# A quarter of w_mod's gate section by four transfers of four partitions, loaded at the start into the first row of the query weights, with the second key pair issued behind it

## The chip, the cores and the metric

The kernel runs on one core of one Trainium2 chip. Five engines share it: TensorE (PE, whose weight loads are shown apart as PEld), VectorE (DVE), ScalarE (ACT), GpSimd (POOL) and SyncE (SP, which here issues nearly all the transfers). Sixteen DMA engines move data between memory and the core's buffers. The metric is device time in microseconds (us). The kernel before takes 663.5 us, the median of three runs (663.39 to 663.72).

## The reference

One decode step of an adaptive-layer-norm block, with batch 4 and width 512. A vector c gives six modulation vectors of 512 numbers for each of the four rows; the attention has 32 heads of 128 and a cache of 4096 keys and values; behind it comes a small gated MLP.

```
mod = (silu(c) @ w_mod).reshape(4, 6, 1, 512)        # w_mod: 512 x 3072
sa, ca, ga, sb, cb, gb = the six slices of mod
h = layernorm(x) * (1 + ca) + sa
x = x + ga * attention(h, k_cache, v_cache, wq, wo)  # q = h @ wq; softmax(q k / sqrt(128)) v @ wo
h = layernorm(x) * (1 + cb) + sb
z = gelu(h @ w_in);  z1, z2 = halves of z;  g = w_sp * layernorm(z2) + b_sp
x = x + gb * ((z1 * g) @ w_out)
```

The last of the six slices, gb, is the gate section: columns 2560 to 3071 of w_mod. It is used only in the last line.

## The kernel before, in words

The caches are 4 x 32 x 4096 x 128 numbers of two bytes each, 134 MB for the keys and 134 MB for the values. They pass once through three buffers of 64 KB in each of the 128 partitions: bufA and bufB take the keys in turn, bufC the values. Step i of the main loop (L680) handles four heads of one batch row; steps pair up, so that one load of 8.39 MB serves two of them. The last two steps, N0 = 30 and L = 31, are handled singly, with smaller loads; the values of step 31 come in four pieces of 64, 32, 16 and 16 columns (`TAIL`, L20).

The order of the work on every engine is the order of the program text (L93, a manual schedule). A wait is put in where an instruction touches bytes that another has not finished with.

At the start (L115 to L159) the query weights (32 KB of each partition) and w_mod's first five sections go into bufC, which is free until the first values arrive. SP issues in this order: query weights, w_mod's five sections, the first key pair in two halves (`load_k(0)`), and the second key pair (`load_k(2)`, into bufB, not used before). The rows of c and x and two single numbers go by ACT's queue. From c the kernel makes cT (L254 to L264): four transposes, silu, and a cast to bf16; column j of cT holds elements j, j+4, j+8 ... of c, since w_mod is read as `(p j) n -> p j n`.

`mod_rows` (L269) multiplies cT by sections of w_mod and leaves rows; `mod_turn` (L280) transposes them to columns. Sections 0 and 1 are needed at once for h; then `queries` (L316) makes the 32 heads' queries in eight turns. Sections 2, 3 and 4 are multiplied behind the queries (L367), and turned and stored as modT by `late_mod_b` (L353), which step 0 calls behind its second multiplication.

The gate section is loaded last of all: `load_end` (L588) issues the last output weights, w_in, w_out, and then the gate section in four transfers (`KG`, L22), one for each j: 128 partitions x 1 KB. They go into `wg_sb` in bufC. At the very end of the kernel, sixteen matmuls (L870) multiply it by cT into the tile `gb`, behind the 28 matmuls of w_out (L862), whose result is y. DVE combines y with the statistics of z2 (L890 to L901) and multiplies by gb (L902). A transpose (L904), one addition (L906) and the store follow.

SP's issues at the end also wait, one by one, for a transfer some places ahead of them to land. They are the first four pieces of the last values for w_out and the gate section's first transfers.

```
    load_k(0)
    load_k(2)
    ...
        for ks in KG:
            nc.sync.dma_start(out=wg_sb[:, ks], in_=wm[:, ks, 5 * D:])
```

Of the kernel before, what the change touches and what calls it, by code (L numbers as in the profile page):

```python
# [8 lines left out]
BF16 = mybir.dt.bfloat16  # L9
F32 = mybir.dt.float32  # L10
# [8 lines left out]
RD = 8  # L19
TAIL = (64, 32, 16, 16)  # L20
KIN = (slice(0, 2), slice(2, 4))
KG = tuple(slice(k, k + 1) for k in range(4))  # L22
JW = (slice(0, 4), slice(4, 7))
RW = (slice(0, 4), slice(4, 8))

# [26 lines left out]
def kernel(  # L52
# [16 lines left out]
    nc = tc.nc  # L69
    P = 128  # L70
    B, _, D = A_x.shape
# [3 lines left out]
    DJ = D // P  # L75
# [4 lines left out]
    R = P // HQ  # L80
# [15 lines left out]
    ident_bf = front.tile([P, P], BF16, name="ident_bf")  # L96
# [3 lines left out]
    bufA, bufB, bufC = bufs  # L100
    consts = ctx.enter_context(tc.tile_pool(name="consts", bufs=1))
    wk = ctx.enter_context(tc.tile_pool(name="work", bufs=2))
    psum = ctx.enter_context(tc.tile_pool(name="psum", bufs=1, space=PSUM))
    KB = 1024
# [4 lines left out]
    def ps_sm(shape, dtype=F32):  # L109
        return psum.tile(shape, dtype, name="sm", bufs=3)  # L110

    def ps_q():
        return psum.tile([P, 512], F32, name="qps", bufs=1)
# [3 lines left out]
    pre = Arena(bufC, 52 * KB, 64 * KB)  # L117
    c_sb = pre.tile([B, D], BF16, name="c_sb")
# [5 lines left out]
    wm = w_mod.rearrange("(p j) n -> p j n", p=P)  # L124
# [21 lines left out]
    def load_k(i):  # L146
        if i < N0:
            load(bufs[i // 2 % 2], kv_view(A_k_cache, i), (NJ, NJ) if i == 0 else (NP,))
        else:
            load(kts[i], kv_view(A_k_cache, i), (NJ,))  # L150
# [5 lines left out]
            load(vts[i], kv_view(A_v_cache, i), TAIL if i == L else (NJ,))  # L156

    load_k(0)
    load_k(2)  # L159

    make_identity(nc, ident_bf)
    ident_f = consts.tile([P, P], F32, name="ident_f")
# [16 lines left out]
    def spread(n, pattern, axis, **sizes):  # L179
# [18 lines left out]
        out=far, in0=half, scalar1=-1.0, scalar2=-NEG, op0=ALU.add, op1=ALU.mult  # L198
    )
    nc.gpsimd.tensor_scalar(  # L200
        out=fars, in0=far[:, :, None].to_broadcast([P, 2, R // 2]), scalar1=-1.0, scalar2=None, op0=ALU.mult
    )
    cT = consts.tile([P, DJ, B], BF16, name="cT")
    pbd8 = consts.tile([P, NP, HP], BF16, name="pbd")
    nc.gpsimd.memset(pbd8, 0.0)
    pbds = pbd8.rearrange("p n q -> p (n q)").rearrange("p (k n q) -> p k n q", k=4, q=HQ)
# [5 lines left out]
    def rows_to_cols(src):  # L212
        t = ps_sm([P, DJ, B], BF16)
        for j in range(DJ):
            nc.tensor.transpose(t[:, j, :], src[0:B, j:D:DJ], ident_bf[0:B, 0:B])
        return t
# [34 lines left out]
        rsqrt(rs, v, 1.0, eps)  # L251
        return xc, rs

    cps = rows_to_cols(c_sb)  # L254
    cx = pre.tile([P, DJ, B], F32, name="cx")
    nc.vector.tensor_copy(out=cx, in_=cps)
    sg = pre.tile([P, DJ, B], F32, name="sg")
    nc.vector.tensor_scalar(
        out=sg, in0=cx, scalar1=-60.0, scalar2=-1.0, op0=ALU.max, op1=ALU.mult
    )  # L260
# [5 lines left out]
    mrows = pre.tile([P, D], F32, name="mrows")  # L266
# [13 lines left out]
    def mod_turn(n):  # L280
        mps = ps_sm([P, DJ, n * R])
        for j in range(DJ):
            nc.tensor.transpose(mps[:, j, :], mrows[0:n * R, j:D:DJ], ident_f[0:n * R, 0:n * R])  # L283
        return mps.rearrange("p j (s r) -> p s j r", s=n)[:, :, :, 0:B]
# [57 lines left out]

    for n in range(2 * B):
        queries(n)

    sp_t = pre.tile([1, 2], BF16, name="sp_t")
    nc.scalar.dma_start(out=sp_t[:, 0:1], in_=B_w_sp[0:1, 0:1])
    nc.scalar.dma_start(out=sp_t[:, 1:2], in_=B_b_sp.rearrange("(a b) -> a b", b=1))
    modT = consts.tile([P, 3 * DJ, B], F32, name="modT")
    g8 = consts.tile([P, 2, B], F32, name="g8")  # L350
    spf = consts.tile([P, 2], F32, name="spf")

    def late_mod_b():  # L353
        mps = mod_turn(3)
        sps = ps_sm([P, 2])
        nc.tensor.matmul(sps, lhsT=ones_b, rhs=sp_t, start=True, stop=True)
        nc.vector.tensor_copy(
            out=modT.rearrange("p (s j) b -> p s j b", s=3),
            in_=mps,
        )  # L360
        nc.vector.tensor_copy(out=spf, in_=sps)
        nc.gpsimd.tensor_copy(out=g8[:, 1, :], in_=spf[:, 0:1].to_broadcast([P, B]))
        cbT = modT[:, 2 * DJ:3 * DJ, :]
        nc.gpsimd.tensor_scalar_add(out=cbT, in0=cbT, scalar1=1.0)
# [210 lines left out]
    wol_sb = Arena(bufC, 0, 8 * KB).tile([P, HP, D], BF16)  # L575
    win_sb = Arena(bufC, 8 * KB, 22 * KB).tile([P, DJ, F], BF16)
    wout_sb = Arena(bufC, 22 * KB, 29 * KB).tile([P, NH, D], BF16)
    wg_sb = Arena(bufC, 29 * KB, 33 * KB).tile([P, DJ, D], BF16)
    tl = Arena(bufC, 33 * KB, 64 * KB)
    NL = GP * HP * DH  # L580

# [6 lines left out]
    def load_end():  # L588
        wol = A_wo[NL:H * DH].rearrange("(p r) n -> p r n", p=P)
        for rs in RW:  # L590
            nc.sync.dma_start(out=wol_sb[:, rs], in_=wol[:, rs])
        win = B_w_in.rearrange("(p j) n -> p j n", p=P)
        for ks in KIN:
            nc.sync.dma_start(out=win_sb[:, ks], in_=win[:, ks])
        for js in JW:
            nc.sync.dma_start(
                out=wout_sb[:, js],
                in_=B_w_out[js.start * P:js.stop * P].rearrange("(p j) n -> p j n", p=P),
            )
        for ks in KG:  # L600
            nc.sync.dma_start(out=wg_sb[:, ks], in_=wm[:, ks, 5 * D:])

    acc = late.tile([P, DJ, B], F32, name="acc")
    st2 = late.tile([P, 2, B, DJ + 1], F32, name="st2")
# [75 lines left out]
    for i in range(NT):  # L680
        mult(i, 0)
        if i >= 1:
            scores(i - 1)
        for k in normed_in(i - 1):
            norm_b(k)
        pick = i - 3 if i % 2 == 0 and i >= 4 else None
        if i % 2 and 3 <= i < L:
            pv(i - 2)
        if i % 2 and i < N0:
            load_v(i)  # L690
        reduce_d(i, 0)
        if pick:
            o_pick(pick)
            o_cols(pick)
        if i == L - 1:
            deal(0)
        if i == L:
            deal(2)
            pv(N0 - 1)
            load_end()  # L700
            nc.gpsimd.memset(pbd8, 0.0)  # L701
            nc.vector.memset(opss[1], 0.0)
            exps(N0)
        mult(i, 1)
        if i == 0:
            late_mod_b()
        for k in normed_in(i):
            norm_r(k)
        if pick:
            o_scale(pick)  # L710
        sum8(i, 0)
        if i == L - 1:
            dealt(0)
        if i == L:
            dealt(1)
            dealt(2)
            o_pick(N0 - 1)
            nc.vector.memset(opss[0], 0.0)
        reduce_d(i, 1)
        sum_rest(i)  # L720
        for k in normed_in(i):
            norm_a(k)
        if i == L - 1:
            deal(1)
        if i == L:
            o_cols(N0 - 1)
            project()
        if i % 2 and i + 3 < N0:
            load_k(i + 3)
        elif i == N0 - 3:  # L730
            load_k(N0)
            load_k(L)
        elif i == N0 - 1:
            load_wo()
            load_v(N0)
            late_consts()
        elif i == N0:
            load_v(L)
# [89 lines left out]
    def gate(h, part):  # L828
# [26 lines left out]
        out=zz.rearrange("p f g b -> p g b f"), in0=z1[:, None].to_broadcast([P, 2, B, NH]),  # L855
        in1=st3[:, 0:2], op=ALU.mult,
    )
    y = ps_q()[:, 0:DJ * 2 * B].rearrange("p (j g b) -> p j g b", j=DJ, g=2)
    for js in JW:
        for j in range(DJ):  # L860
# [3 lines left out]
                    start=(j == 0 and f == 0), stop=(f == NH - 1), skip_group_check=True,  # L864
                )

    gb = ps_sm([P, DJ, B])
    for k in range(DJ):
        for j in range(DJ):
            nc.tensor.matmul(  # L870
                gb[:, j, :], lhsT=wg_sb[:, k, j * P:(j + 1) * P], rhs=cT[:, k, :],
                start=(k == 0 and j == 0), stop=(k == DJ - 1), skip_group_check=True,
            )
    mq3 = tl.tile([P, 2, B], F32, name="mq3")
    nc.vector.tensor_reduce(
# [62 lines left out]
```

## Time and profile before

| what | value |
|---|---|
| median of three runs | 663.5 us (663.39 to 663.72) |
| the profiled execution | 663.53 us |
| its span | 661.7 us |
| DVE busy | 570.8 us, 86% |
| PE busy | 316.3 us, 48% |
| ACT busy | 172.0 us, 26% |
| POOL busy | 19.4 us, 3% |
| bytes moved by DMA | 283.07 MB, mean 428 GB/s |
| mean granted clock of TensorE | 0.747 |

The span is the time from the first to the last thing that the profiler recorded; the execution's own time is 1.83 us longer. The page's line "DMA" gives, for 40 equal slices of the span, the mean busy share of the 16 DMA engines in tenths (9 is 90% or more). A transfer is recorded as packets, each with a queue (q1 is SP's, q10 is ACT's, q8 and q14 carry instructions for the engines themselves), a start, a size and a duration; every DMA engine that takes part in a transfer writes a packet of four bytes when its share is done. In the timeline a row is: start, duration, engine, line, operation, output and inputs, count, and in brackets the idle time before it and what ended it.

### The profile page before, as it was taken

The page shows a single profiled execution, that of the slowest core. Times are in us where ns is not written, and L with a number is a line of the kernel's source. Part 1 is how long each engine was busy: PE and PEld are TensorE (multiplying, and loading weights), DVE is VectorE, ACT ScalarE, POOL GpSimd, SP SyncE. Part 2 cuts the span into 40 slices and gives each one's busy share as a digit, 9 for nine tenths or more (in the row PEclk, how much of TensorE's full clock was granted, in tenths as well). Part 3 has the DMA queues.
Part 4 walks back from the last instruction along what each step waited for, and adds up shares of the span by engine and source line. Part 5 has one row for each costly group of instructions (what it writes and reads, how often), then busy time and mean ns, then how long its engine had stood idle before and what let it go on. Part 6 is the DMA issues. An engine that isn't in the chain of part 4 may idle for free.

```text
span 661.7 us, 5060 instructions
## 1 busy us (share of the span) xinstructions
PE 316.3 (48%) x2064; PEld 134.6 (20%) x2064; DVE 570.8 (86%) x368; ACT 172.0 (26%) x284; POOL 19.4 (3%) x56
## 2 busy tenths in 40 slices
PE   1565363635154463514446351444535254453885
PEld 0122121212021121202112120111212022121444
DVE  3239999999898998989899898979979898999943
ACT  1220505033060603206060330605023060503322
POOL 3000000000000000000000000000000000030100
PEclk9998787867678785767878576787856778775975
DMA  8999999999999999999999999999999999999996
GB/s 364 447 427 444 440 441 440 441 405 436 440 433 440 444 433 412 445 432 432 437 440 437 424 436 428 433 440 440 429 432 433 428 440 441 420 422 451 414 417 280
DMA packets 8060, 283.07 MB, mean 428 GB/s; under 512 B 860, under 2 KB 1380, under 8 KB 2916
## 3 DMA queue, kind: packets, MB, share of 16 engines
q1 hardware_dynamic: 8016, 282.73, 99.0%
q8 instruction: 16, 0.26, 0.1%
q14 instruction: 8, 0.07, 0.0%
q10 hardware_dynamic: 20, 0.01, 0.0%
HBM read 282.73 MB, written 0.00 MB: 427 GB/s over the span
## 4 chain that ended last, share of the span: by engine, by line
DMA 70%; PE 14%; DVE 10%; ACT 4%; issue 1%; POOL 0%; SPq 0%; ACTq 0%; DVEq 0%
DMA bC<-in_A_v_cache_dram 54%; PE ops L510 11%; DMA bA<-in_A_k_cache_dram 6%; DMA bC<-in_A_wo_dram 4%; DVE S L401 4%; DMA bC<-in_w_mod_dram 4%; DVE bA L381 3%; ACT pbd L455 3%; PE red L389 2%; DMA bC<-in_B_b_sp_dram 2%; DVE bB L381 1%; DVE S L412 1%; PE qps L331 1%; PE sm L323 1%; ACT qbp L341 0%
## 5 line engine op out<-in xcount | busy, mean ns | idle before, releaser
L455 ACT ACTIVATE pbd<-S,nb 32x256 bf16<-32x256 f32 x120 | 154.3, 1520 | 422.6 <-DVE nb L442 421.3
L381 DVE TENSOR_TENSOR bA<-bA,qbp 128x8192 bf16<-128x8192 bf16 x32 | 142.4, 4451 | 21.7 <-DMA bA<-in_A_k_cache_dram 21.7
L389 PE MATMUL red<-bB,ident_bf 128*128 128x512 bf16 x344 | 97.2, 441 | 113.6 <-DVE bB L381 113.6
L389 PE MATMUL red<-bA,ident_bf 128*128 128x512 bf16 x332 | 93.3, 440 | 110.2 <-DVE bA L381 110.2
L389 PEld LDWEIGHTS <-ident_bf 128*128 128x128 bf16 x676 | 72.8, 110 | 337.7 <-issue 175.5
L381 DVE TENSOR_TENSOR bB<-bB,qbp 128x8192 bf16<-128x8192 bf16 x28 | 123.7, 4418 | 13.4 <-DMA bB<-in_A_k_cache_dram 13.4
L510 PE MATMUL ops<-bC,pbd 128*32 128x512 bf16 x960 | 83.6, 525 | 69.9 <-DMA bC<-in_A_v_cache_dram 64.8
L401 DVE TENSOR_REDUCE S<-bA 128x48 f32<-128x6144 bf16 x15 | 98.1, 6543 | 0.0
L401 DVE TENSOR_REDUCE S<-bB 128x48 f32<-128x6144 bf16 x14 | 91.6, 6542 | 0.0
L510 PEld LDWEIGHTS <-pbd 128*32 128x32 bf16 (+1 forms) x1016 | 37.4, 126 | 120.5 <-issue 63.9
L455 ACT ACTIVATION_READ_ACCUMULATOR pbd<-S,nb 32x1 f32 x120 | 58.8, 490 | 0.0
L412 DVE TENSOR_REDUCE S<-red 128x64 f32<-128x512 f32 x64 | 43.7, 683 | 4.4 <-PE red L389 4.3
L469 POOL TENSOR_TENSOR rsb<-maskd,rs 128x8 f32<-128x8 f32 x15 | 3.8, 253 | 556.9 <-ACT pbd L455 556.9
L381 DVE TENSOR_TENSOR bB<-bB,qbo 128x8192 bf16<-128x8192 bf16 x4 | 17.6, 4410 | 0.0
L522 DVE TENSOR_REDUCE osb<-ops 128x128 f32<-128x512 f32 x17 | 11.8, 692 | 0.6
L519 DVE TENSOR_TENSOR ops<-ops,m 128x512 f32<-128x512 f32 x15 | 10.4, 693 | 0.0
L295 DVE SCALAR_TENSOR_TENSOR bC<-sm,bC 128x16 f32<-128x16 f32 x1 | 0.2, 175 | 11.4 <-PE sm L283 11.4
L488 PE MATMUL sm<-rsb,inv_d 128*128 128x32 f32 (+2 forms) x12 | 2.9, 338 | 14.6 <-POOL rsb L469 14.6
L273 PE MATMUL sm<-bC,cT 128*4 128x512 bf16 x20 | 3.7, 621 | 8.4 <-DMA bC<-in_w_mod_dram 8.4
L455 ACT ACTIVATE pbd<-S,nM 32x128 bf16<-32x128 f32 x8 | 4.6, 576 | 12.1 <-POOL pbd L701 10.9
L425 DVE TENSOR_REDUCE mrow<-S 128x1 f32<-128x256 f32 (+1 forms) x17 | 6.9, 404 | 0.6
L331 PE MATMUL qps<-bC 128*128 128x256 bf16 (+1 forms) x16 | 4.5, 383 | 4.1 <-ACT qbp L341 2.8
(159 smaller groups left out, 134.0 us busy)
## 6 DMA issues: line engine op xcount, KB each, us to landing
bA<-in_A_k_cache_dram SPq DMA_DIRECT2D x2, 4096.0 KB, 31.4
bB<-in_A_k_cache_dram SPq DMA_DIRECT2D x2, 4096.0 KB, 41.6
bC<-in_A_wq_dram SPq DMA_DIRECT2D x1, 4096.0 KB, 12.3
bA<-in_A_v_cache_dram SPq DMA_DIRECT2D x1, 4096.0 KB
bA<-in_A_wo_dram SPq DMA_DIRECT2D x1, 3072.0 KB
bC<-in_w_mod_dram SPq DMA_DIRECT2D x1, 2560.0 KB, 18.0
bB<-in_A_v_cache_dram SPq DMA_DIRECT2D x1, 2048.0 KB, 32.3
bC<-in_B_w_in_dram SPq DMA_DIRECT2D x2, 896.0 KB
```

Of the source, the lines that this page charges most:

```text
L323: nc.tensor.matmul(qr[R * q:R * (q + 1)], lhsT=hT[:, k, :], rhs=wq_v[:, k, gs, q, :], start=(k == 0), stop=(k == DJ - 1), tile_position=(0 ...
L331: nc.tensor.matmul(qp[:, 0:npair], lhsT=eb2[k][:, b].rearrange("p k q r -> p (k q r)"), rhs=qrow[:, h, k:2 * npair:2], start=(k == 0), sto ...
L381: nc.vector.tensor_tensor(out=kt, in0=kt, in1=bc(q, KC), op=ALU.mult)
L389: nc.tensor.matmul(red, lhsT=ident_bf, rhs=kt[:, :, m * rd:(m + 1) * rd], start=(m == 0), stop=(m == DH // rd - 1),)
L401: nc.vector.tensor_reduce(out=st[i, "S"][:, n0:NJ], in_=kts[i][:, n0:NJ, :], axis=AX.X, op=ALU.add)
L412: nc.vector.tensor_reduce(out=st[i, "S"][:, kc * KC:kc * KC + on_pe(i, kc)], in_=st.pop((i, "red", kc)), axis=AX.X, op=ALU.add,)
L425: nc.vector.tensor_reduce(out=mrow, in_=S, axis=AX.X, op=ALU.max)
L455: nc.scalar.activation(out=pbd8[r, :, 2 * q + h] if pair(i) else pbds[r, i % 4, :, q], in_=S[r, :], func=AF.Exp, bias=nM[r, h:h + 1], scal ...
L469: nc.gpsimd.tensor_tensor(out=st["P", g, "rsb"][:, b], in0=maskd[:, :, None].to_broadcast([P, HQ, 2]), in1=rs[:, None, :].to_broadcast([P, ...
L510: nc.tensor.matmul(ops_of(i)[g:g + rows], lhsT=pb[:, n, :], rhs=vt[:, n, :], start=(m < 4), stop=(m >= end - 4), tile_position=(0, g),)
L519: nc.vector.tensor_tensor(out=ops, in0=ops, in1=sel[:, :, None].to_broadcast([P, G, DH]), op=ALU.mult)
L522: nc.vector.tensor_reduce(out=osb, in_=ops.rearrange("p g d -> p d g"), axis=AX.X, op=ALU.add)
```

## The change

The gate section has 512 rows. The first 384 are still loaded at the end, now in three transfers (`KE` = 3) of 128 partitions x 1 KB. The other 128 rows are loaded at the start: 16 partitions (`PU`) of 8 rows (`RU`) each, that is 8 KB for each of 16 partitions, into the place where the first row (j = 0) of the query weights has been. Four transfers carry them, the b-th with partitions b, b+4, b+8 and b+12. They are issued by SP behind the queries in the program text, and `load_k(2)` is moved from the head of the kernel to stand behind them.

cT gets 15 columns in place of 4: the old four, three for the 384 rows in their new order, and eight for the 128 rows, of which only 16 partitions are used (the rest of the tile is cleared by POOL). That makes fifteen transposes in place of four, and two copies out of PSUM in place of one. In step 0 a new function, `mod_uneven`, multiplies the 128 rows' part with eight matmuls of 512 columns into rows 96 to 99, and ACT copies it to `mrows` with its columns reordered; `late_mod_b` turns four sections in place of three, and modT becomes a third larger. At the end one f32 matmul with the identity puts that part into `gb`, now ahead of y's matmuls, and twelve matmuls in place of sixteen add the rest behind y.

```diff
-KG = tuple(slice(k, k + 1) for k in range(4))
+KE = 3
+RU = 8
+EV = 128 * KE
+PU = 16
+KG = tuple(slice(k, k + 1) for k in range(KE))
...
     load_k(0)
-    load_k(2)
+    wgu_sb = Arena(bufC, 0, RU * KB).tile([P, RU, D], BF16)[0:PU]
...
-    cT = consts.tile([P, DJ, B], BF16, name="cT")
+    NC = DJ + KE + RU
+    cT = consts.tile([P, NC, B], BF16, name="cT")
...
-    cps = rows_to_cols(c_sb)
-    cx = pre.tile([P, DJ, B], F32, name="cx")
-    nc.vector.tensor_copy(out=cx, in_=cps)
-    sg = pre.tile([P, DJ, B], F32, name="sg")
+    cps = ps_sm([P, NC, B], BF16)
+    cuts = [slice(j, D, DJ) for j in range(DJ)]
+    cuts += [slice(k, EV, KE) for k in range(KE)] + [slice(EV + r, D, RU) for r in range(RU)]
+    for n, cut in enumerate(cuts):
+        pn = P if n < DJ + KE else PU
+        nc.tensor.transpose(cps[0:pn, n, :], c_sb[0:B, cut], ident_bf[0:B, 0:B])
+    cx = pre.tile([P, NC, B], F32, name="cx")
+    nc.gpsimd.memset(cx[:, DJ + KE:], 0.0)
+    nc.vector.tensor_copy(out=cx[:, 0:DJ + KE], in_=cps[:, 0:DJ + KE])
+    nc.vector.tensor_copy(out=cx[0:PU, DJ + KE:], in_=cps[0:PU, DJ + KE:])
+    sg = pre.tile([P, NC, B], F32, name="sg")
...
     for n in range(2 * B):
         queries(n)
+    wu = w_mod[EV:D, 5 * D:].rearrange("(p r) n -> p r n", r=RU)
+    for b in range(4):
+        nc.sync.dma_start(out=wgu_sb[b:PU:4], in_=wu[b:PU:4])
+    load_k(2)
...
-    modT = consts.tile([P, 3 * DJ, B], F32, name="modT")
+    modT = consts.tile([P, 4 * DJ, B], F32, name="modT")
...
+    def mod_uneven():
+        mp = ps_sm([P, D])
+        for r in range(RU):
+            nc.tensor.matmul(
+                mp[3 * R:3 * R + B], lhsT=cT[0:PU, DJ + KE + r, :], rhs=wgu_sb[:, r, :],
+                start=(r == 0), stop=(r == RU - 1), tile_position=(0, 3 * R),
+            )
+        nc.scalar.copy(
+            out=mrows[3 * R:3 * R + B].rearrange("b (p j) -> b j p", j=DJ),
+            in_=mp[3 * R:3 * R + B].rearrange("b (j p) -> b j p", j=DJ),
+        )
...
-        mps = mod_turn(3)
+        mps = mod_turn(4)
...
-    wg_sb = Arena(bufC, 29 * KB, 33 * KB).tile([P, DJ, D], BF16)
+    wg_sb = Arena(bufC, 29 * KB, 33 * KB).tile([P, KE, D], BF16)
...
+        wge = w_mod[0:EV, 5 * D:].rearrange("(p k) n -> p k n", p=P)
         for ks in KG:
-            nc.sync.dma_start(out=wg_sb[:, ks], in_=wm[:, ks, 5 * D:])
+            nc.sync.dma_start(out=wg_sb[:, ks], in_=wge[:, ks])
...
         if i == 0:
+            mod_uneven()
             late_mod_b()
...
+    gb = ps_sm([P, DJ, B])
+    nc.tensor.matmul(
+        gb.rearrange("p j b -> p (j b)"), lhsT=ident_f, rhs=modT[:, 3 * DJ:4 * DJ, :].rearrange("p j b -> p (j b)"),
+        start=True, stop=False, skip_group_check=True,
+    )
     y = ps_q()[:, 0:DJ * 2 * B].rearrange("p (j g b) -> p j g b", j=DJ, g=2)
...
-    gb = ps_sm([P, DJ, B])
-    for k in range(DJ):
+    for k in range(KE):
         for j in range(DJ):
             nc.tensor.matmul(
-                gb[:, j, :], lhsT=wg_sb[:, k, j * P:(j + 1) * P], rhs=cT[:, k, :],
-                start=(k == 0 and j == 0), stop=(k == DJ - 1), skip_group_check=True,
+                gb[:, j, :], lhsT=wg_sb[:, k, j * P:(j + 1) * P], rhs=cT[:, DJ + k, :],
+                start=False, stop=(k == KE - 1), skip_group_check=True,
             )
```

More of the change, by code (lines that the diff above doesn't have):

```diff
@@ L357, in late_mod_b @@
         nc.vector.tensor_copy(
-            out=modT.rearrange("p (s j) b -> p s j b", s=3),
+            out=modT.rearrange("p (s j) b -> p s j b", s=4),
             in_=mps,
```

## The prediction

> **What bounds the kernel now.** I read the page's DMA lines first, then the DMA packet records of the trace, then the timeline at both ends, then the chain that ended last.
>
> ```profile
> span 661.7 us, 5060 instructions
> ...
> DMA  8999999999999999999999999999999999999996
> ...
> q1 hardware_dynamic: 8016, 282.73, 99.0%
> q8 instruction: 16, 0.26, 0.1%
> q14 instruction: 8, 0.07, 0.0%
> q10 hardware_dynamic: 20, 0.01, 0.0%
> ```
>
> SP's transfers (q1) fill the 16 DMA engines from 1.7 us to the last slice. In the packet records each 8.39 MB load ends 19.32 us after the one before it (57.07, 76.39, 95.71 ... 578.68 on the earliest engine): no gap anywhere. So work on the other engines in the middle costs nothing; a byte in the stream does.
>
> The 16 engines are not level. The four-byte completion packets of a transfer lie 0.48 us apart at 37.75 us, but 3.33 us apart at 634.38 us. Each step is one instruction-fetch packet: a q8 fetch (16 KB) puts its engine back 1.42 us, a q14 fetch (8 KB) 0.55 to 0.85 us. The 16 q8 fetches go round eight engines; the other eight get only the q14 ones. Now to the engines that matter. The loads of c and x (4 rows of 1 KB each) have left 4 data and 4 completion packets each, and the two one-element loads 2 each: 8 + 8 + 4 = the 20 of q10. So a four-partition load ran on four engines. Matching the x packets to the q1 packets on either side, those four had, at 37.75 us, the offsets 0.00, 0.02, 0.11 and 0.30 us. Followed to 634.38 us, they are at 0.00, 1.13, 0.13 and 2.83 us. The last, which I call engine R, took q14 fetches at 103.26, 345.58 and 625.77 us. The latest engine of all is at 3.33.
>
> Timeline of the last 25 us (start, duration, engine, line, [idle before, releaser]):
>
> ```profile
> 638.06 1.03 PE L510 MATMUL ops<-bA,pbd 128*16 128x512 bf16 x8 [0.49 <-DMA bA<-in_A_v_cache_dram]
> ...
> 642.96 1.44 PE L510 MATMUL ops<-bB,pbd 128*16 128x512 bf16 x16 [0.67 <-DMA bB<-in_A_v_cache_dram]
> ...
> 645.41 0.61 PE L510 MATMUL ops<-bB,pbd 128*16 128x512 bf16 x8 [0.69 <-DMA bB<-in_A_v_cache_dram]
> ...
> 646.63 0.56 PE L544 MATMUL qps<-pbd,bB 128*128 128x4 bf16 x16 [0.61 <-DMA bB<-in_A_v_cache_dram]
> ...
> 655.96 0.68 PE L220 MATMUL sm<-bA 128*128 128x56 f32 x2
> ...
> 656.61 0.89 PE L862 MATMUL qps<-bC 128*128 128x8 bf16 x28
> ...
> 657.35 1.19 PE L870 MATMUL sm<-cT,bC 128*128 128x4 bf16 x16
> ...
> 657.53 0.19 DVE L890 TENSOR_TENSOR bC<-g,qps 128x32 f32<-128x32 f32 x1 [0.18 <-PE qps L862]
> ...
> 658.24 0.17 DVE L901 TENSOR_TENSOR bC<-bC 128x16 f32<-128x16 f32 x1
> ...
> 658.58 0.17 DVE L902 TENSOR_TENSOR bC<-bC,sm 128x16 f32<-128x16 f32 x1 [0.16 <-PE sm L870]
> ```
>
> Each piece of the last V load ends a PE wait; behind the third there are 12 us of dependent compute. Two paths meet at L902: that compute (L901 ends 658.41) and w_mod's gate section, whose last packet ends 657.90. The chain shows how:
>
> ```profile
> 650.42 7.81 DMA bC<-in_w_mod_dram
> 658.23 0.04 issue
> 658.27 0.28 PE sm L870 x4
> 658.55 0.02 issue
> 658.58 0.18 DVE bC L902
> ```
>
> The transfer path wins by about 0.13 us only. And the landing of the last V pieces is set by the **latest** of the 16 engines.
>
> **The change part by part.** Sum against the profiled execution: 663.53 us, span 661.7 and 1.83 around it; the median is 663.5.
>
> *Tail, 128 KB less.* In the packet records an engine takes 0.345 us for one of the four gate transfers (8 packets of 1 KB and a completion). With one fewer, the last packet of an unmoved engine ends at 657.55. At L902 this can return at most the 0.13 us by which that path leads.
>
> *Front, 128 KB more.* Four transfers of four partitions, 8 rows of 1 KB for each. By the x row, each runs on four engines, the same four: 4 x 8 = 32 packets of 0.043 us and 4 completions, 32/8 x 0.345 = 1.38, say 1.40 us on each of four engines and nothing on twelve. The Trainium skill, "DMA: Bandwidth & Descriptors", section "Why a DMA increments its semaphore by 16 and not by 1", has this as a rule: the engine count is the largest k up to 16 that divides the slowest dimension on both sides, on SP and ACT queues the lowest-numbered k. The 20 packets of q10 agree. Three of the four engines have room (0.00, 0.13, 1.13, with 1.40 added still under 3.33). Engine R hasn't: 2.83 + 1.40 = 4.23. Until 617 us R is at 1.99 + 1.40 = 3.39, level with 3.33, so the middle does not move. From V's last two transfers on, R sets the landings:
>
> ```
> completion, us      earliest engine   engine R   latest   R + 1.40
> V of step 30                 634.38     637.21   637.71     638.61
> V of step 31, piece 1        639.25     642.08   642.57     643.48
> piece 3                      642.95     645.79   646.28     647.19
> piece 4                      644.20     647.03   647.53     648.43
> gate section, last           654.58     657.40   657.90     658.80 (658.46 with one transfer less)
> ```
>
> Each landing is 0.90 us later. PE waits for each of them today (0.49, 0.67, 0.69, 0.61 us, all ended by the DMA), so the compute moves by the whole 0.90: **+0.90 us**.
>
> *The last gate product.* Four L870 matmuls go (4 x 0.026 us, behind y; not on the path any more). In their place one f32 matmul with ident_f stands **before** the 28 y matmuls (L862). The f32 matmul of the same kind at L550 takes 0.447 us from its start to the start of the bf16 matmul behind it (647.541 to 647.986). L220's pair lets its follower load weights at 656.215 and finish that at 656.485; y began at 656.608, when DVE had made zz. With the new one from 656.485, y starts at 656.93: +0.32 us, which DVE's L890 to L901 pass on whole. Bounds: 0 if it fits the gap, 0.45 if nothing overlaps. I take 0.32, as the rows around it give it. L901 then ends at 658.73 and L902 starts at about 658.77, 0.19 us later than today, no longer held by the gate section: **+0.19 us**. With the 0.90 the gate's last product is ready near 659.2, still ahead of DVE at 659.63.
>
> *The move of the second key pair (SP's queue).* It now waits behind four transfers that wait for the last reader of the query weights' row 0: the first four of the second L323 group (29.99 us, 16 matmuls in 1.90 us), so about 30.6. Row 0 alone counts: at the end the output weights' first half is issued at 622.64 into the first 8 KB of a buffer whose other part PE reads until 625.8. Four issues at 0.4 to 0.65 us and the pair's own 0.48 end by 33.7. Issue to first packet is 1.03 us (0.73 to 1.76), so the pair is there by 34.7. The stream reaches it at 37.75 on the earliest engine: 3 us of cover, **cost 0**; without the cover see the rivals. Behind it on SP is the first V load, issued at 48.30 and needed at 57.07: 8 us of cover.
>
> *Front compute, all covered.* Eleven more transposes and one more DVE copy, a POOL clear behind the 1.81 us clear at 3.54, wider sigmoid: cT later by some 2 us, xn with it (11.9 to about 14); PE waits for w_mod until 19.21. Eight more row products (L273: 8 in 1.87 us), one ACT copy (0.58) and wider transposes fall between 42.3 and 48.0, where PE waits for the one-element loads. Without that cover PE would be 3 us later at step 0, while the stream stays the bound: 0.
>
> Sum: 663.53 + 0.90 + 0.19 = 664.62, against the median **664.6 us**, 0.17% longer.
>
> **Rivals.** My bound for no change is 0.2%, about what a measurement of this kernel can tell: 662.2 to 664.8.
>
> *A hole in the stream (slower).* If the four transfers wait for all query work (PE L336 ends 36.31) and not for row 0, four issues (1.8 us) and 1.03 us put the pair's first packet at 39.1, against 37.75: a hole of 1.35 us for the whole stream, in which R's extra packets hide. 663.53 + 1.35 + 0.19 = 665.1. It decides from a hole of 1.15 us on. For it: SP is in order. Against: the 622.64 issue.
>
> *Even spread.* If 32 rows are dealt over 16 engines, each is 0.35 later in front: 663.53 + 0.35 + 0.19 = 664.1. The x load had only four rows and can't exclude it.
>
> *R not late.* If R's third fetch moves behind V, R is at 3.39, landings hold, and 663.53 + 0.19 = 663.7. R's fetch stands in the trace at 625.77; which instruction calls it, no view says.
>
> *Small gain.* The f32 matmul fits the gap and R isn't late: 663.53 - 0.13 = 663.4. A gain over 0.2% has no place to come from: L901 at 658.41 stands.
>
> *Each small transfer pays a start.* If the four engines idled 1.03 us (issue to first packet) ahead of each, R would be 4.1 later still: 668.7. The gate transfers, as small per engine, follow each other without a gap, which speaks against it. The Trainium skill, "DMA: Bandwidth & Descriptors", section "Rules for kernel authors", says that transfers under 64 KB are mostly overhead; these are 32 KB.
>
> **How the numbers follow.** Forecast 0.57 (664.2 to 665.0: L550's bounds and 0.2 us on the landings), hole 0.13, even spread 0.10, R not late 0.11, small gain 0.05, starts 0.04. The range 663.6 to 665.5 leaves out the small gain, the starts, and the upper part of the hole. Slower by over 0.2% (above 664.83): the hole, the starts, and a third of the forecast, whose middle lies only 0.2 us below the bound: 0.36. Faster by over 0.2%: no case gives it; 0.04 for what I don't see. Same: 0.60.
>
> **What would show it.** In the packets: 128 more of 1 KB near 38 us on four engines, 128 fewer at the end; completions of the V pieces some 0.9 us further apart. In the timeline: L544's DMA wait ends near 647.5; y starts at 657.8; L902 is no longer released by PE. The second pair's packets follow the first's without a gap, or there is the hole. I am wrong if those four engines are not the x load's four, or if R's fetch is elsewhere.

## The result and the profile after

The changed kernel takes 664.79 us (median; 664.53 to 665.19), the kernel before in the same series 663.46 us: ratio 1.0020, 95% interval 1.0013 to 1.0027. It is slower by 1.33 us, which lies just inside the 0.2% (664.83) that the prediction took as its bound for no change. The forecast was 664.6, with a range of 663.6 to 665.5. The profiled execution took 664.66 us, 1.13 us more than that of before.

The page of the changed kernel, at its span, the DMA line of part 2 and part 3:

```profile
span 662.9 us, 5104 instructions
...
DMA  8999999999999999999999999999999999999996
...
q1 hardware_dynamic: 8016, 282.73, 98.8%
q8 instruction: 16, 0.26, 0.1%
q14 instruction: 8, 0.07, 0.0%
q10 hardware_dynamic: 20, 0.01, 0.0%
```

Bytes and packets are what they were; the stream still fills every slice, and the span has grown by 1.2 us. So the time isn't in the amount of work. The timeline of SP's queue about the moved load (start, duration, queue, line):

```profile
30.61 2.80 SPq L359 DMA_DIRECT2D bC<-in_w_mod_dram  x4
33.45 0.44 SPq L147 DMA_DIRECT2D bB<-in_A_k_cache_dram  x1
```

The four transfers are issued from 30.61 us, as soon as row 0 of the query weights is read, and the second key pair at 33.45. In the packet records, 128 packets of 1 KB run from 37.73 to 39.30 us, 32 on each of exactly four engines; the other twelve go from the first key pair to the second (first packet at 37.69) with nothing between. No hole.

The last 25 us of the changed kernel, from the timeline (lines answer to those of before as L510 to L538, L544 to L572, L862 to L897, L870 to L904, L890 to L924, L901 and L902 to L935 and L936, and the MLP's first matmul L836 to L866; L889 is new):

```profile
638.92 1.03 PE L538 MATMUL ops<-bA,pbd 128*16 128x512 bf16 x8 [1.45 <-DMA bA<-in_A_v_cache_dram]
...
643.77 1.30 PE L538 MATMUL ops<-bB,pbd 128*16 128x512 bf16 x16 [0.61 <-DMA bB<-in_A_v_cache_dram]
...
646.22 0.61 PE L538 MATMUL ops<-bB,pbd 128*16 128x512 bf16 x8 [0.83 <-DMA bB<-in_A_v_cache_dram]
...
647.43 0.56 PE L572 MATMUL qps<-pbd,bB 128*128 128x4 bf16 x16 [0.60 <-DMA bB<-in_A_v_cache_dram]
...
654.76 1.86 PE L866 MATMUL red<-bC 128*128 128x4 bf16 x56 [1.04 <-DVE bC L845]
...
656.70 0.68 PE L225 MATMUL sm<-bA 128*128 128x56 f32 x2
...
657.17 0.57 PE L889 MATMUL sm<-modT,ident_f 128*128 128x16 f32 x2
...
657.57 0.89 PE L897 MATMUL qps<-bC 128*128 128x8 bf16 x28
...
659.21 0.17 DVE L935 TENSOR_TENSOR bC<-bC 128x16 f32<-128x16 f32 x1
...
659.49 0.17 DVE L936 TENSOR_TENSOR bC<-bC,sm 128x16 f32<-128x16 f32 x1
...
660.44 0.36 SPq L941 DMA_DIRECT2D out_dram<-bC  x1
```

Two rows of the timeline of before that belong beside these:

```profile
654.02 1.86 PE L836 MATMUL red<-bC 128*128 128x4 bf16 x56 [0.98 <-DVE bC L815]
...
659.53 0.36 SPq L907 DMA_DIRECT2D out_dram<-bC  x1
```

Against before, the four waits for V pieces end 0.86, 0.81, 0.81 and 0.80 us later (638.06, 642.96, 645.41 and 646.63 there). The MLP's first matmul (L866) starts 0.74 later, y 0.96, L935 0.97, L936 0.91, and the store's issue 0.91. So most of the loss is made by 638.9 us, in the landings; about 0.2 more is added between L866 and y: 2.81 us from the one to the other, 2.59 before.

The end of the chain that ended last, of the changed kernel (start, duration, what):

```profile
657.37 0.36 PE sm L889 x2
657.73 0.74 PE qps L897 x28
658.50 0.20 DVE bC L924
...
659.21 0.18 DVE bC L935
...
659.49 0.18 DVE bC L936
```

The transfer of w_mod's gate section, 7.81 us of the chain before, is gone from it; the new f32 product L889 is in it, and L936 has no releaser any more.

The completions in the packet records say which engine holds the landings. Step 30's V load, 16 engines (us):

```
before   earliest 634.38 ... 637.21 (R) ... 637.49, 637.71
after    earliest 634.50 ... 637.53, 637.60, 638.45 (R)
```

Engine R, whose fetches stand at 102.08, 346.82 and 625.79 us here, has gone from a place in the pack to the last by 0.85 us. Its packets can be followed one by one. At the end of the first key pair R is at 37.91 us here and at 38.05 before, so it starts 0.14 earlier. Its share of the four small transfers ends at 39.29, 1.38 later. At the second key pair it is 1.24 behind its place before (58.61 against 57.37), and at 638.45 still 1.24; the three fetches cost it the same in both kernels.

One part of the loss appears only behind the store. The store is issued 0.91 us later, the profiled execution ends 1.13 later. At the end of the program SP waits for its semaphores one by one, in a fixed order. Its records (start, us; the store's own is marked):

```
before   659.935  659.999  660.061  660.125  660.919 (store's)  done 660.984
after    660.850 (store's, lasts 0.977)  661.863  661.925  661.989  662.051  done 662.116
```

The transfers of SP and ACT take eight semaphores in turn (the records name them), and with another number of transfers the store has another one. Before, four waits were passed while the store was under way and its own came behind them; after, the store's comes first and four of 0.063 us follow it: from issue to done 1.45 us before, 1.68 after, some **0.22 us** that no view of the profile lists.

So the profiled difference has three terms: landings +0.74 (as L866 feels them), the product before y +0.22 with 0.06 returned because L902 no longer waits for the gate section, and the order of the last waits +0.22. Their sum is 1.12, against 1.13. The medians differ by 1.33, with an interval of 0.9 to 1.8 us; the 0.2 between the two figures is within it and isn't traced.

### The profile page after: what moved, and what is told of

It is laid out like the page before. It is cut to its first block, busy times and chain, and to the rows that moved or that the text cites. A ratio compares the mean times of both kernels' runs of the same rounds, so it can differ in the third digit from the quotient of the medians.

```text
span 662.9 us, 5104 instructions
## 1 busy us (share of the span) xinstructions
PE 318.2 (48%) x2081; PEld 135.0 (20%) x2081; DVE 569.9 (86%) x369; ACT 173.2 (26%) x285; POOL 19.5 (3%) x57
## 4 chain that ended last, share of the span: by engine, by line
DMA 61%; DVE 21%; PE 13%; ACT 2%; issue 1%; SPq 0%; ACTq 0%; DVEq 0%
DMA bC<-in_A_v_cache_dram 40%; DMA bA<-in_A_k_cache_dram 12%; PE ops L538 8%; DVE S L429 7%; DVE bA L409 7%; DMA bB<-in_A_v_cache_dram 5%; DVE bB L409 3%; PE red L417 3%; DMA bC<-in_w_mod_dram 3%; DMA bC<-in_B_b_sp_dram 2%; ACT pbd L483 2%; DVE S L440 1%; PE qps L343 1%; PE sm L335 1%; DVE osb L550 0%
## 5 line engine op out<-in xcount | busy, mean ns | idle before, releaser
L417 PE MATMUL red<-bA,ident_bf 128*128 128x512 bf16 x332 | 94.8, 446 | 109.1 <-DVE bA L409 109.1
L538 PE MATMUL ops<-bC,pbd 128*32 128x512 bf16 x960 | 81.8, 516 | 69.5 <-DMA bC<-in_A_v_cache_dram 60.7
L538 PEld LDWEIGHTS <-pbd 128*32 128x32 bf16 (+1 forms) x1016 | 36.4, 124 | 120.2 <-issue 63.1
L550 DVE TENSOR_REDUCE osb<-ops 128x128 f32<-128x512 f32 x17 | 11.8, 692 | 0.6
```

What stands on the lines that cost most here:

```text
L417: nc.tensor.matmul(red, lhsT=ident_bf, rhs=kt[:, :, m * rd:(m + 1) * rd], start=(m == 0), stop=(m == DH // rd - 1),)
L538: nc.tensor.matmul(ops_of(i)[g:g + rows], lhsT=pb[:, n, :], rhs=vt[:, n, :], start=(m < 4), stop=(m >= end - 4), tile_position=(0, g),)
L550: nc.vector.tensor_reduce(out=osb, in_=ops.rearrange("p g d -> p d g"), axis=AX.X, op=ALU.add)
```

## The experiments

My theory after the comparison: the landings are late because the four-partition transfers put 1.4 us on four engines, one of them R, while the same bytes on other engines cost nothing; the product costs 0.22; the last waits cost 0.22 to 0.25. The rivals: the load costs in front, whichever engines carry it (even spread, or a hole); or the loss comes from the tail's new compute. Times below are medians with those of the kernel before on the same chip.

| experiment | us | before | difference | ratio, 95% interval |
|---|---|---|---|---|
| load alone, four transfers | 664.69 | 663.59 | +1.10 | 1.0007 to 1.0025 |
| half the rows, four engines | 664.10 | 663.64 | +0.46 | 0.9998 to 1.0016 |
| half the rows, two engines | 664.06 | 663.59 | +0.47 | 0.9998 to 1.0016 |
| product earlier | 664.48 | 663.64 | +0.84 | 1.0004 to 1.0022 |
| store's semaphore alone | 663.88 | 663.59 | +0.29 | 0.9995 to 1.0012 |
| engine R alone | 664.30 | 663.59 | +0.71 | 1.0002 to 1.0020 |
| one transfer | 664.95 | 663.64 | +1.31 | 1.0011 to 1.0028 |
| load alone, one transfer, adjacent | 664.96 | 663.59 | +1.37 | 1.0011 to 1.0029 |
| load alone, one transfer, spread | 664.43 | 663.59 | +0.84 | 1.0004 to 1.0021 |
| six transfers | 668.12 | 663.64 | +4.48 | 1.0054 to 1.0079 |
| eight transfers of two partitions | 669.33 | 663.59 | +5.74 | 1.0073 to 1.0101 |
| the same, product earlier | 668.99 | 663.59 | +5.40 | 1.0068 to 1.0096 |

An interval is about 1 us wide, so differences of a few tenths between two experiments are read from their traces, not from this table.

### The load alone

The kernel before, its tail untouched, with four transfers like the change's in front of the second key pair; what they bring is not read, and the whole gate section still comes at the end.

```
-    load_k(2)          # behind load_k(0)
     for n in range(2 * B):
         queries(n)
+    wgu_sb = Arena(bufC, 0, 8 * KB).tile([P, 8, D], BF16)[0:16]
+    wu = w_mod[3 * P:D, 5 * D:].rearrange("(p r) n -> p r n", r=8)
+    for b in range(4):
+        nc.sync.dma_start(out=wgu_sb[b:16:4], in_=wu[b:16:4])
+    load_k(2)
```

> The kernel before with one part of the change alone: the four transfers of four partitions in front, behind the queries, with the second key pair behind them. The 128 rows are loaded twice, nothing reads the first copy. Theory: R ends step 30's values 0.74 us later than the latest did, as in the changed kernel; L902 waits for R's last gate packet, near 659.4; the store's semaphore is checked first, 0.22: 0.9 to 1.0 us longer, 664.4 us. Rival (the front load is hidden, the compute edits cost the time): 663.5 to 663.7 us.

It came out 1.10 us longer. The timeline of this kernel at the V waits and at the meeting of the two paths:

```profile
638.76 1.03 PE L514 MATMUL ops<-bA,pbd 128*16 128x512 bf16 x8 [0.80 <-DMA bA<-in_A_v_cache_dram]
...
647.27 0.56 PE L548 MATMUL qps<-pbd,bB 128*128 128x4 bf16 x16 [0.61 <-DMA bB<-in_A_v_cache_dram]
...
659.14 0.17 DVE L906 TENSOR_TENSOR bC<-bC,sm 128x16 f32<-128x16 f32 x1 [0.19 <-PE sm L874]
```

The V waits end 0.70 and 0.64 us later than before, and the gate section's matmuls (L874) release L906 as they released L902. The load alone, without any of the new compute, makes most of the loss (0.80 us in the profiled execution, where the change shows 1.13). The four extra transfers have also moved the store's semaphore to the front of the last waits, as in the change.

### Half the rows, on four engines or on two

Both bring 64 rows instead of 128 and leave the other 64 out. The first halves what each of the four engines gets; the second keeps 32 packets per engine but uses two partitions for a transfer.

```
     for b in range(4):
-        nc.sync.dma_start(out=wgu_sb[b:PU:4], in_=wu[b:PU:4])
+        nc.sync.dma_start(out=wgu_sb[b:PU:4, 0:RU // 2], in_=wu[b:PU:4, 0:RU // 2])
```
```
-        nc.sync.dma_start(out=wgu_sb[b:PU:4], in_=wu[b:PU:4])
+        nc.sync.dma_start(out=wgu_sb[b:8:4], in_=wu[b:8:4])
```

> The changed kernel with the four transfers kept, each carrying four of its eight rows per partition; the other 64 rows of the gate section are left out. Theory: engine R gets 16 packets, 0.70 us instead of 1.40, ends step 30's values at 637.75, just behind the others at 637.60: 0.70 us earlier, 664.1 us. Rival (each small transfer has a cost of its own, not its packets): four transfers as before, 664.8 us.

> The changed kernel with four transfers of two partitions, 8 rows each: 64 packets on two engines, 32 on each, so those two carry what each of four carries in the changed kernel; the other 64 rows of the gate section are left out. No more transfers than in the changed kernel, so no later second key pair. Theory (R alone sets the landings): if R is not among the two, the latest engine ends step 30's values at 637.60 and the time is 0.85 us below the changed kernel, 0.5 us above the one before. If R is one of the two: as the changed kernel, 1.3 us above. Rival (32 packets of 1 KB on any engine in front are enough): 1.3 us above, with R not carrying any.

Both are some 0.47 us above before, about what the product and the last waits cost by themselves. In the second the packets are on exactly two engines, 32 on each, as many per engine as in the change (their second key pair begins at 39.10 and 39.35 us). Step 30's V load is complete at 637.74 us, against 637.71 before and 638.45 in the changed kernel; in the first at 637.80. From the timeline of the two-engine kernel:

```profile
645.47 0.61 PE L538 MATMUL ops<-bB,pbd 128*16 128x512 bf16 x8 [0.20 <-DMA bB<-in_A_v_cache_dram]
...
646.65 0.57 PE L572 MATMUL qps<-pbd,bB 128*128 128x4 bf16 x16 [0.57 <-DMA bB<-in_A_v_cache_dram]
```

The last V wait ends at 646.65, and at 646.63 before. So 1.4 us of packets in front cost nothing at the end when the engines that carry them are not the late one. That R isn't among these two shows in the packets: the engine that takes the fetch at 103.14 us, R's by its time (103.26 before, 102.08 in the change), is then 0.3 us behind the earliest engine, and the two that carried the packets are 1.5 and 1.7 behind. That speaks against the rivals in which the load costs by its place in front: with half the bytes they would have half the loss in the landing, which moved by 0.03 us. The first of the two kernels fits as well: R with half the load is at 2.83 + 0.70 = 3.53 by the prediction's working, only 0.20 behind the latest engine of before.

### The product earlier

The f32 product stands ahead of the MLP's first matmuls, where PE waits for DVE.

```
+    gb = ps_sm([P, DJ, B])
+    nc.tensor.matmul(
+        gb.rearrange("p j b -> p (j b)"), lhsT=ident_f, rhs=modT[:, 3 * DJ:4 * DJ, :].rearrange("p j b -> p (j b)"),
+        start=True, stop=False, skip_group_check=True,
+    )
     x1s = tl.tile([B * DJ, P], F32, name="x1s")
...
-    gb = ps_sm([P, DJ, B])
-    nc.tensor.matmul(
-        gb.rearrange("p j b -> p (j b)"), lhsT=ident_f, rhs=modT[:, 3 * DJ:4 * DJ, :].rearrange("p j b -> p (j b)"),
-        start=True, stop=False, skip_group_check=True,
-    )
     y = ps_q()[:, 0:DJ * 2 * B].rearrange("p (j g b) -> p j g b", j=DJ, g=2)
```

> The changed kernel with the f32 identity product moved from ahead of y's matmuls to ahead of the MLP's first matmuls, where PE waits for DVE. Theory: y starts as soon as zz is made, 0.22 us earlier, and L935 ends that much earlier: 664.55 us. Rival (the product fits a gap of PE and costs nothing): 664.8 us.

Timeline of this kernel:

```profile
653.92 0.61 PE L854 MATMUL sm<-modT,ident_f 128*128 128x16 f32 x2
655.02 1.85 PE L871 MATMUL red<-bC 128*128 128x4 bf16 x56 [0.49 <-DVE bC L845]
...
657.60 0.89 PE L897 MATMUL qps<-bC 128*128 128x8 bf16 x28
```

From the first MLP matmul to y it is 2.58 us, as before the change (2.59), against 2.81 with the product in its place. L871 still waits 0.49 us for DVE, so the product is covered. Its price is 0.22 to 0.23. In this profiled execution R's landing was 638.72, 0.27 later than in the changed kernel's, so the spans don't show the gain; the intervals of the medians don't separate it either.

### The store's semaphore, and engine R alone

First: the kernel before with three one-element loads on ACT's queue at the start, which move the store to another semaphore and do nothing else. Second: the change, with the product early as above, and five such loads, so that the store's semaphore is waited for last.

```
     nc.scalar.dma_start(out=x_sb, in_=A_x.rearrange("b s d -> (b s) d"))
+    spare = pre.tile([1, 4], BF16, name="spare")
+    for k in range(3):
+        nc.scalar.dma_start(out=spare[:, k:k + 1], in_=B_w_sp[0:1, 0:1])
```
```
+    spare = pre.tile([1, 8], BF16, name="spare")
+    for k in range(5):
+        nc.scalar.dma_start(out=spare[:, k:k + 1], in_=B_w_sp[0:1, 0:1])
```

> The kernel before with three more one-element loads at its start, on ACT's queue, into bytes that nothing reads. The count of transfers is then that of the changed kernel, and the store gets the semaphore that SP checks first at the end, with four more checks behind it. Theory: 0.22 us longer, 663.68 us. Rival (what the span shows behind the store is chance): 663.46 us.

> The changed kernel with its two smaller costs taken away: the f32 product ahead of the MLP, and five more one-element loads at the start, so that the store gets the semaphore that SP checks last. Theory (three terms: engine R, the product 0.22, the final checks 0.25): only engine R is left, 0.8 to 0.9 us above the kernel before. Rival (the terms do not add, another cost hides behind): over 1.1 us above.

In the first, SP's first wait ends at 661.10 us and four more follow, to 661.36: the order is that of the changed kernel. The time is 0.29 longer, but its interval (-0.3 to +0.8 us) holds nothing as well, so the time alone doesn't show the 0.22; the records of SP do (1.68 us from the store's issue to done, as in the changed kernel). In the second the first waits are passed between 660.486 and 660.676 us and the store's own ends last, at 661.45 (1.45 us from issue to done, as before). What is left of the change there is R: 638.34 for the latest completion, and from its timeline

```profile
638.81 1.03 PE L541 MATMUL ops<-bA,pbd 128*16 128x512 bf16 x8 [1.06 <-DMA bA<-in_A_v_cache_dram]
...
654.64 1.84 PE L874 MATMUL red<-bC 128*128 128x4 bf16 x56 [0.50 <-DVE bC L848]
...
657.20 0.89 PE L900 MATMUL qps<-bC 128*128 128x8 bf16 x28
```

the first V wait 0.75 us later than before, L874 0.62 later, y 0.59. The whole is +0.71 us. Adding the product (0.22) and the last waits (0.22) gives 1.15, near the 1.13 of the profiled executions and the 1.33 of the medians (0.9 to 1.8 us by the interval). Within the intervals, the terms add.

### The same rows by one transfer

If four engines are the trouble, all sixteen should be the cure: one transfer of sixteen partitions puts eight packets on each engine.

```
-    for b in range(4):
-        nc.sync.dma_start(out=wgu_sb[b:PU:4], in_=wu[b:PU:4])
+    nc.sync.dma_start(out=wgu_sb, in_=wu)
```

> The changed kernel with its quarter sent by one transfer of 16 partitions instead of four of four. Theory (engine R carries 32 packets and sets V's landings): 8 packets, 0.35 us, fall on every engine; R ends the load of step 30's values at 637.4 instead of 638.45 and the other late engines at 637.95, so the landings come 0.50 us earlier. With three transfers fewer the store's semaphore is again the last that SP checks: another 0.22 us. 664.79 - 0.72 = 664.05 us. Rival (a longer stream or SP's wait in front costs the time, not one engine): only the 0.22 goes, 664.55 us.

A miss: 1.31 us over before, no better than the change. The V load of step 30 was complete at 639.11, later than with R alone. I then gave the kernel before such a load by itself, once into sixteen adjacent partitions and once into every eighth; nothing reads it.

```
-    load_k(2)          # behind load_k(0)
     for n in range(2 * B):
         queries(n)
+    wgu_sb = Arena(bufC, 0, 8 * KB).tile([P, 8, D], BF16)
+    wu = w_mod[3 * P:D, 5 * D:].rearrange("(p r) n -> p r n", r=8)
+    nc.sync.dma_start(out=wgu_sb[0:16], in_=wu)       # second kernel: wgu_sb[0:P:8]
+    load_k(2)
```

> The kernel before with only a front load added: one transfer of 16 adjacent partitions (0 to 15), 8 packets of 1 KB on each engine, behind the queries with the second key pair behind it; nothing reads it. In the one-transfer run every engine's first packet of the second key pair took 3.0 to 3.4 us instead of 2.42. If that comes from 16 engines writing 16 adjacent partitions, it is here again: 0.35 + 0.8 us on every engine, and two checks behind the store's (0.13): 1.2 to 1.3 us above the kernel before. If it was chance: 0.35 + 0.13, 0.5 us above.

> The same with the one transfer's 16 partitions eight apart (0, 8 ... 120), the same packets and bytes. Theory (adjacent partitions are what is crowded): the first key packets take 2.42 us, 0.5 us above the kernel before. Rival (1 KB packets on all 16 engines at once in mid-stream are slow wherever they go): as with adjacent partitions, 1.2 us above.

From the packet records (us; "pair done" is the second key pair's completions on the engines, with one later engine in brackets):

```
                        1 KB packet   first 64 KB of an engine   pair done               V of step 30
changed kernel              0.046             2.42               57.00 (earliest)           638.45
one transfer                0.056          2.55 to 3.36          58.01 to 58.52 (60.38)     639.11
load alone, adjacent        0.062          2.88 to 3.71          58.14 to 59.15 (59.82)     639.35
load alone, every eighth    0.048          2.57 to 2.72          57.59 to 58.17 (59.68)     638.48
```

With one transfer, not only the small packets are slow, but the first 64 KB packets of the key pair behind them: all sixteen engines lose time there, 0.1 to 0.9 us each (0.5 to 1.3 with the load alone). The packets behind these take 2.42 us again. With the partitions eight apart the slowing is smaller but still there (+0.84 us in all, between the two values that I had expected). So by the packets adjacency is most of it and not all; the intervals of the two medians overlap.

The slowing isn't peculiar to transfers into sixteen partitions. The first packets of the query weights at the start of the kernel, 32 KB each, took 1.23 to 2.18 us before the change, and later ones of that size 1.21. Behind the hole of the six transfers below, the first 64 KB packets took 2.93 to 3.36 us. In each of these cases all sixteen engines come to large packets anew; in the changed kernel twelve of them go straight on from the first key pair, and nothing is slowed. What the engines contend for isn't shown, and stays open.

### Six transfers, and eight of two partitions

Two more transfers in the same manner, into partitions that nothing reads, should put 0.69 us more on R. Eight transfers of two partitions should take the rows to two engines without R.

```
         nc.sync.dma_start(out=wgu_sb[b:PU:4], in_=wu[b:PU:4])
+    wgx_sb = Arena(bufC, 0, RU * KB).tile([P, RU, D], BF16)[PU:2 * PU]
+    for b in range(2):
+        nc.sync.dma_start(out=wgx_sb[b:PU:4], in_=wu[b:PU:4])
```
```
-    for b in range(4):
-        nc.sync.dma_start(out=wgu_sb[b:PU:4], in_=wu[b:PU:4])
+    for b in range(8):
+        nc.sync.dma_start(out=wgu_sb[b:PU:8], in_=wu[b:PU:8])
```

> The changed kernel with two more transfers of four partitions of the same rows, into 16 partitions that nothing reads. Theory: 16 packets more on the four engines, 0.70 us, all of it on V's landings since R is the latest already: R ends step 30's values at 639.15. The store's semaphore moves from the first to the second wait, 0.06 us back: 665.4 us. Rival (the landings are not what moved the end): 664.8 us. Rival (SP too late for the second key pair): SP issues 1.4 us more, the pair is there near 36.5, still ahead of 37.7, no hole.

> The changed kernel with eight transfers of two partitions instead of four of four: all 128 packets on two engines, 64 each, 2.76 us. Theory: if R is not one of the two, R ends step 30's values at 637.05, and the two, which take few or no fetches, stay below the others at 637.60: landings 0.85 us earlier, and the store's semaphore is checked fourth instead of first (0.19): 663.75 us. If R is one of the two: 1.36 us later, 666 us. Rival (SP): eight issues of 0.7 us end near 36.2, the second key pair's first packet comes near 37.7, just when the stream needs it; a hole would be some tenths at most.

> Both edits together on the changed kernel: two engines (eight transfers of two partitions) and the f32 product ahead of the MLP. Theory: 663.75 - 0.22 = 663.5 us, level with the kernel before, since its compute path to L901 was only 0.13 us ahead of the gate section. Rival (the moved quarter is worth more than 0.13 us once it is off engine R): below 663.3 us.

The last is the eight transfers with the product early, as above. All three missed by several microseconds, for one reason. The timeline of the kernel with six transfers, SP's queue and then the last V wait:

```profile
30.62 2.79 SPq L359 DMA_DIRECT2D bC<-in_w_mod_dram  x4
33.45 5.69 SPq L362 DMA_DIRECT2D bC<-in_w_mod_dram  x2
40.28 0.34 SPq L147 DMA_DIRECT2D bB<-in_A_k_cache_dram  x1
...
651.20 0.56 PE L575 MATMUL qps<-pbd,bB 128*128 128x4 bf16 x16 [0.63 <-DMA bB<-in_A_v_cache_dram]
```

The sixth issue waited until 38.52 us, because its semaphore, one of the eight, belonged to the second half of the first key pair, which was complete only at 38.50. The key pair behind it then waited for the next semaphore in turn, that of a one-element load of ACT's queue, which landed at 40.27. So it was issued at 40.28 instead of 33.45, its first packet is at 41.25 instead of 37.7, and for about 3.5 us the stream of the caches stood still. SP's waits in this kernel show both (us in total, how often, the longest):

```profile
SPq L362 <- DMA bA<-in_A_k_cache_dram: 4.4, 1, 4.4
...
SPq L147 <- DMA bC<-in_B_w_sp_dram: 1.1, 1, 1.1
```

The last V wait ends 3.8 us later than in the changed kernel: the hole arrives whole at the end. With eight transfers the sixth issue waits so until 38.78 us and the seventh, for the one-element load, until 40.26:

```profile
30.70 10.83 SPq L359 DMA_DIRECT2D bC<-in_w_mod_dram  x8
41.58 0.40 SPq L147 DMA_DIRECT2D bB<-in_A_k_cache_dram  x1
```

The pair's first packet is at 42.61, a hole of 4.9 us, and the span is 4.8 us longer than the changed kernel's. The early product takes 0.34 off again, within the intervals. So none of these kernels tells anything of R, and the two-engine question had to be put again with four transfers (above).

No version came out faster than the kernel before. All that the gate section could return was 0.13 us at L902, and each way of bringing its rows in front cost more than that somewhere.

## Why the prediction was right, and where its sizes were off

The forecast's case came true in its mechanism: 664.79 against 664.6, by landings that one engine sets and a product before y. Point by point:

- **Front, four engines, R among them:** right. The packets were on four engines, 32 on each, and R became the last. The rule cited there from the Trainium skill, "DMA: Bandwidth & Descriptors", section "Why a DMA increments its semaphore by 16 and not by 1", agrees with all three widths run: four partitions went by four engines, two by two, sixteen by sixteen. Which engines they are by number isn't in the records.
- **+0.90 on the landings:** mis-sized. R's completion went from 637.21 to 638.45, 1.24 later where I had added 1.40; the V waits moved by 0.80 to 0.86, L866 by 0.74, and with R alone the whole time by 0.71. R's own packets took 1.38, which I had rounded up, and R began them 0.14 earlier than in the kernel before, where I had left its place as it was. That is the whole 0.16; its three fetches cost the same as before.
- **+0.32 for the f32 product:** mis-sized, it measured 0.22. I had it begin 0.525 us after L220's pair and y 0.447 behind it, by L550; L889 began 0.47 after L225 and y 0.40 behind it.
- **-0.13 at the tail:** the gate section did leave the chain, and L936 has no releaser, as forecast. What returned is 0.06, since L936 starts 0.28 us behind L935's start where the other DVE steps take 0.21.
- **Second key pair, cost 0:** right here, its issue ended at 33.89 where 33.7 was the forecast, and there was no hole. But the reason for it was incomplete. I saw the wait for row 0 and not the wait for a semaphore: with six transfers in front the hole was 3.5 us, more than twice the rival's 1.35. The rival "a hole in the stream" had the right place and the wrong cause.
- **Front compute, cost 0:** right. The half-row kernels keep all of it and their V load lands within 0.1 us of before.
- **Even spread at 664.1:** not what happened, and mispriced besides. The rows dealt over sixteen engines cost 664.95, since 0.35 us per engine was not all: the packets slowed one another and the stream behind them.
- **R not late, at 663.7:** excluded; R's third fetch came at 625.79 us, ahead of step 30's V landing, as the forecast had it.
- **Starts of small transfers at 668.7:** excluded. The Trainium skill, "DMA: Bandwidth & Descriptors", section "Rules for kernel authors", calls transfers under 64 KB mostly overhead; here four of 32 KB took 1.38 us on an engine, back to back at 0.046 us a packet, so this trace doesn't bear that out for transfers that are queued behind others.
- **Missing altogether:** the order of SP's last waits, +0.22. Without it the profiled execution would have been near 664.44, 0.2 under the forecast; the overestimates of the first two terms and this omission nearly cancelled (0.90 + 0.19 forecast, 0.74 + 0.16 + 0.22 measured). That the total came closer than its parts is luck.

## What to carry to other kernels

When a stream bounds a kernel and compute waits for its last pieces, the landing is that of the latest DMA engine: before adding a transfer over few partitions, find from the packet records which engines will carry it and how far each is behind at the end. Thirty-two kilobytes on a late engine cost 0.7 us here, the same on two early ones nothing. And count the transfers that are issued ahead of a large one: once the eight semaphores that SP and ACT share here were in use, the next issues waited for older transfers to land, and that left holes of 3.5 to 4.9 us in the stream.

## What of the hardware I had not expected

- A transfer into sixteen partitions in mid-stream slowed the next packet of every engine: the first 64 KB packets took 2.88 to 3.71 us with adjacent partitions and 2.57 to 2.72 with every eighth, against 2.42 behind four-partition transfers. Behind a hole in the stream they were as slow (2.93 to 3.36 us).
- The end of the program isn't free of the number of transfers: SP's last waits take 0.063 us each in a fixed order, and whether the store's came first or last moved the end by 0.22 to 0.25 us.
- The engines' drift was alike from kernel to kernel: with four transfers of all the rows, step 30's V load was complete at 638.45 us (the change), 638.72 (product early), 638.28 (the load alone) and 638.34 (R alone), against 637.71 before. A late engine that looks accidental in one trace could be counted on here, to about 0.4 us; each value is from one profiled execution.
